# Attention and two feed-forward layers on one core: reciprocals broadcast per head, sums of exponentials on POOL, six weight chunks moved

## Chip, cores, metric

One Trainium2 chip, of which the kernel uses one core. The metric is the device time of one execution in microseconds, the median of several runs. The engines are named as in the profile: PE (matmul), PEld (its weight loads), DVE (vector), ACT (scalar), POOL (GpSimd), SP (the queue that issues the DMAs).

## What is computed

Attention over 4 batches of 8 heads with 576 positions and 64 channels (the mask is causal, a bias comes from a running sum of s), a feed-forward layer with softplus, and a gated one with an RMS norm in front. The second softmax denominator has a small constant added; the change touches where.

```python
scores = scale * np.matmul(q, k.transpose(0, 1, 3, 2))
cum = np.cumsum(np.maximum(s, 0.0), axis=-1)
bias = -(cum[:, :, :, None] - cum[:, :, None, :])
scores = np.where(causal, -1000000000.0, scores + np.minimum(bias, 0.0))
attn = np.exp(scores - np.max(scores, axis=-1, keepdims=True))
attn = attn / (np.sum(attn, axis=-1, keepdims=True) + 1e-09)
x = np.matmul(attn, v)             # then (2304, 512): tokens by channels of all heads
h = x @ w_in                       # 512 -> 2048
x = (np.maximum(h, 0.0) + np.log1p(np.exp(-np.abs(h)))) @ w_out
xn = x / np.sqrt(np.mean(x * x, axis=-1, keepdims=True) + 1e-06) * rms_g
g = xn @ w_gate                    # 512 -> 1536
return (g / (1 + np.exp(-g)) * (xn @ w_val)) @ w_out2
```

## The kernel before

The kernel has three stages. **Attention** works on 16 pairs of heads. **The first feed-forward layer** takes 96 steps: six tiles of 384 tokens by six of the sixteen blocks of hidden channels, and then the same tiles by the other ten. **The gated layer** takes 72 steps. Matmuls of single precision are done as three products of a high and a low half (mm3, lines 771 to 774), so each weight is split in two.

The weights lie in memory as float64. A *chunk* of 128 x 512 of them is fetched as 64-bit words (w_fetch, 512 KB), turned into float32 by ACT (w_conv_a, lines 246 and 247), DVE (w_conv_d, lines 253 to 257) and POOL (w_conv_p, line 263), and then either split and kept (w_hi, w_lo) or stored to memory for later (w_store, 256 KB). There are 32 chunks for the first layer and 36 for the second. While attention runs, 12 of the first and N2 = 10 of the second are converted; the remaining 20 and 26 are converted during the first feed-forward layer, the latter one in every OFF2["CV"] = 2.3 steps.

One pair of heads goes through this: q and k are loaded (a_load, line 378) into one of four buffers, two pairs deep; PE transposes them (line 396), ACT and DVE split them into high and low halves (407, 412). A first, coarse product gives scores (a_one, 449) from which DVE takes the row maxima (472); these are transposed (480), copied and put by a small DMA into the operand aq (489, 490). A second, precise product with the maxima folded in (a_two, 505) is turned into exponentials e by ACT (522). PE multiplies them with v (a_v, 539). For the denominators the blocks of e are first added up into zs (a_a, line 533): one add of 128 x 896 on POOL, one of 128 x 640 and one of 128 x 384 on DVE; PE multiplies zs with ones (a_z, also 539). ACT copies the three PSUM results into xz (a_ox, 575), values in xz[:, 0] and sums in xz[:, 1]. A DMA spreads the sums over 128 partitions (z, line 579), DVE adds 1e-9 and takes reciprocals (583, 584), a DMA writes them to memory (rd, 587), and another reads them back, each head's row into 64 partitions (rb, line 591). POOL multiplies (a_xm, 595), and a DMA stores the product x of the pair (line 599).

The order of all this is not written out. attention_ops lists every operation with engine, duration, latency, dependencies and PSUM banks (names such as LD for the load, ZD for z, ZR for the reciprocals, RS for rd, BC for rb, XM for the product, XW for its store, DM for the maxima); attention_order takes them one by one, always the one that could start first by these figures, ties going to the lower rank. The rank is 14.0 per pair plus an entry of the table OFF. Each engine and the SP queue then work through their instructions in that order, and each waits in place where an operand is not ready. SP issues all the DMAs named here. The feed-forward stages are ordered by positions in steps (OFF1, OFF2).

At the end of attention the first two steps of the feed-forward layer (h) stand between the last pairs; the loads of the next token tiles (xr, line 743) stand on SP behind the last store x.

Of the kernel before, what the change touches and what calls it, by code (L numbers as in the profile page):

```python
# [14 lines left out]
AF = mybir.ActivationFunctionType  # L15
# [29 lines left out]
    "PER": 14.0,  # L45
    "LV": -22.71,
    "QT0": 48.88,
    "QH0": -18.02,
    "QL0": -12.77,
    "QT1": 34.64,  # L50
    "QH1": 54.37,
    "QL1": -43.15,
    "AQ": -3.83,
    "RA": -2.83,
    "KA": -0.66,
    "RB": 1.61,
    "KB": -67.40,
    "RC": -33.20,
    "KC": -70.00,
    "RD": -40.04,  # L60
    "MA0": 19.65,
    "MA1": 19.98,
    "MB0": -2.10,
    "MB1": -6.43,
    "MC0": -24.56,
    "MC1": -4.25,
    "MD0": -39.54,
    "MD1": -43.39,
    "MN": 20.02,
    "MT": 9.71,  # L70
    "MH": 24.06,
    "DM": -45.58,
    "Ra": -54.93,
    "Ka": -33.43,
    "Rb": 15.22,
    "Kb": -42.71,
    "Rc": 28.54,
    "Kc": -2.10,
    "Rd": 22.47,
    "Kd": -45.39,  # L80
    "Ea0": -43.42,
    "Ea1": -31.34,
    "Eb0": -34.46,
    "Eb1": 3.11,
    "Ec0": 19.15,
    "Ec1": 24.52,
    "Ed0": -13.92,
    "Ed1": -13.58,
    "A1": 55.11,
    "A2": -55.59,  # L90
    "A3": -54.22,
    "V0": -60.16,
    "V1": -35.91,
    "Z0": -53.57,
    "Z1": 55.74,
    "O0": -58.66,
    "O1": -68.97,
    "O2": 34.39,
    "ZD": -15.00,
    "ZR": 47.90,  # L100
    "RS": -7.46,
    "BC": 47.04,
    "XM": -26.00,
    "XW": -53.74,
    "LD": 10.70,
    "CF": -5.85,
    "CA": 49.36,
    "CD": 70.00,
    "CP": -58.95,
    "CH": 24.21,  # L110
    "CL": 4.79,
    "CS": -55.59,
    "XL": 15.17,
    "X0": -12.63,
    "X1": 20.03,
    "X2": 14.37,
    "X3": 70.00,
    "H0": 5.54,
    "H1": 16.80,
}  # L120
CONV0 = 0.45
CONVR = 0.33
OFF2 = {
    "CV": 2.3,
    "L0": 84.28205,
# [31 lines left out]
def attention_moe_kernel(ctx, tc, q, k, v, s, w_in, w_out, w_gate, w_val, w_out2, rms_g, out):  # L157
# [19 lines left out]
    NA = 2 * FA  # L177
    N2 = 10
    CONV = [(1, c) for c in range(NA)] + [(2, c) for c in range(NA, NA + N2)]
# [345 lines left out]
    def a_a(p, n):  # L525
        e = st["e", p]
        if n == 0:
            st["zs", p] = pools["xo"].tile([P, 2, S - P], F32, tag="zs", name="zs", bufs=2)
        zs = st["zs", p]
        o, x, y, eng = ((zs, e[:, :, P:S], e[:, :, 832:1280], nc.gpsimd),  # L530
                        (zs[:, :, P:], zs[:, :, P:], e[:, :, 1280:1600], nc.vector),
                        (zs[:, :, 2 * P:], zs[:, :, 2 * P:], e[:, :, 576:768], nc.vector))[n]
        eng.tensor_tensor(out=o, in0=x, in1=y, op=ALU.add)

# [32 lines left out]
    def a_ox(p, part):  # L567
        if ("xz", p) not in st:
            st["xz", p] = pools["xo"].tile([P, 2, S], F32, tag="xz", name="xz", bufs=2)
        xz = st["xz", p]  # L570
        if part == 2:
            o, x = xz[:, :, IS:S], st.pop(("x1", p))[:, 0:2 * (S - IS)].rearrange("p (t s) -> p t s", t=2)
        else:
            o, x = xz[:, part, 0:IS], st.pop((("o", "oz")[part], p))[:, 0:IS]
        nc.scalar.activation(out=o, in_=x, func=AF.Copy)

# [4 lines left out]
    def a_zr(p):  # L581
        z = st["z", p]
        nc.vector.tensor_scalar(out=z, in0=z, scalar1=1e-9, scalar2=None, op0=ALU.add)
        nc.vector.reciprocal(out=z, in_=z)

    def a_rd(p):
        nc.sync.dma_start(out=rdd[p].rearrange("h (p c) -> (h p) c", c=9), in_=st.pop(("z", p)))

    def a_rb(p):
        rb = st["rb", p] = pools["xo"].tile([P, S], F32, tag="rb", name="rb", bufs=2)  # L590
        nc.sync.dma_start(out=rb, in_=rdd[p].unsqueeze(1).broadcast_to([2, D, S]))

# [9 lines left out]
    def attention_ops():  # L602
# [8 lines left out]
        for p in range(NP):  # L611
            def add(nm, eng, dur, fn, deps, p=p, **kw):
                op((nm, p), eng, dur, fn, [d if isinstance(d, tuple) else (d, p) for d in deps], p, **kw)

            def old(k, *nms, p=p):
                return [(nm, p - k) for nm in nms] if p >= k else []
# [4 lines left out]
            if p > 1:  # L621
                add("LD", "SP", 1.35, lambda p=p: a_load(p), old(2, "QT0", "QT1"), lat=2.5)
            add("LV", "SP", 1.7, lambda p=p: a_loadv(p), old(3, "V0", "V1"), lat=2.2)
            for w in range(2):
# [16 lines left out]
            add("MH", "ACT", 0.25, lambda p=p: a_mh(p), ["MT"])  # L641
            add("DM", "SP", 1.25, lambda p=p: a_md(p), ["MH", "RA", "RB", "RC", "RD"], lat=2.2)
            for bk, du, ku in (("a", 0.93, 0.11), ("b", 1.32, 0.17), ("c", 0.93, 0.11), ("d", 0.6, 0.11)):
# [16 lines left out]
            add("O1", "ACT", 0.5, lambda p=p: a_ox(p, 1), ["Z0", "O0"])  # L660
            add("O2", "ACT", 0.5, lambda p=p: a_ox(p, 2), ["V1", "Z1", "O0"])
            add("ZD", "SP", 0.62, lambda p=p: a_zd(p), ["O1", "O2"] + old(2, "RS"), lat=2.0)
            add("ZR", "DVE", 0.46, lambda p=p: a_zr(p), ["ZD"])
            add("RS", "SP", 0.35, lambda p=p: a_rd(p), ["ZR"], lat=2.0)
            add("BC", "SP", 0.62, lambda p=p: a_rb(p), ["RS"] + old(2, "XM"), lat=2.2)
            add("XM", "POOL", 1.45, lambda p=p: a_xm(p), ["BC"])
            add("XW", "SP", 0.55, lambda p=p: a_xw(p), ["XM"], lat=2.0)
        for c, (ph, ch) in enumerate(CONV):
            def cv(nm, eng, dur, fn, deps, c=c, ph=ph, ch=ch, **kw):
                op((nm, c), eng, dur, lambda: fn(ph, ch), [d if isinstance(d, tuple) else (d, c) for d in deps],  # L670
                   CONV0 + CONVR * c, **kw)

            def was(nm, k, c=c):
                return [(nm, c - k)] if c >= k else []

            cv("CF", "SP", 0.65, w_fetch, was("CD", 2), lat=5.0)
# [409 lines left out]
```

## Time and profile before

| what | us |
|---|---|
| runs | 1229.65 median of 3 (1229.56 to 1230.39) |
| the profiled execution | 1226.48, its span 1224.7 |
| PE busy | 1120.9 |
| DVE, ACT, POOL busy | 737.2, 560.4, 435.7 |

The span is the time from the first to the last instruction of the profiled execution. Attention fills its first 300 us or so, the first feed-forward layer goes to about 775 us, the gated layer to the end. An engine's busy time counts its own instructions; what it waited for is shown beside the instruction that waited, with an arrow to what released it.

### The profile page before, as it was taken

To read this page: it belongs to the slowest core of one execution; us is meant where nothing else is said; L and a number is where in the kernel's file an instruction comes from. 1 tells how busy PE (TensorE), PEld (TensorE's weight loads), DVE (VectorE), ACT (ScalarE), POOL (GpSimd) and SP (SyncE) were. 2 spreads that over 40 slices of the span, in tenths; PEclk is the share of its full clock that TensorE was granted. 3 is DMA by queue.
4 is the path that set the end of the run, shared out by engine and by line. 5 is a ranking of instruction groups with operands and counts; after the bars stand their busy time and mean duration, and the time that the engine had idled before them with its cause. 6 is when DMAs were issued, how large, how long until landed. Compare 5 with 4: busy or idle time off the path is not lost.

```text
span 1224.7 us, 19418 instructions
## 1 busy us (share of the span) xinstructions
PE 1120.9 (92%) x7428; PEld 1027.6 (84%) x7428; DVE 737.2 (60%) x1218; ACT 560.4 (46%) x1187; POOL 435.7 (36%) x372
## 2 busy tenths in 40 slices
PE   4978887889599989999989988999999999999998
PEld 4756766667588888999989888999999999999997
DVE  5667775544289999889999998433233332333322
ACT  2454544433387887777667666342121111211111
POOL 4466534322265454236567766761000000000000
PEclk9987898997799999999999999999999999999999
DMA  7364566431244343443432332431001010010000
GB/s 172 92 148 122 149 169 169 116 105 44 92 127 136 121 127 123 126 132 101 154 104 60 115 113 63 129 115 63 1 13 39 14 40 1 13 40 13 27 1 27
DMA packets 126493, 107.60 MB, mean 88 GB/s; under 512 B 66528, under 2 KB 112224, under 8 KB 126336
## 3 DMA queue, kind: packets, MB, share of 16 engines
q1 hardware_dynamic: 126368, 106.36, 29.5%
q8 instruction: 58, 0.95, 0.3%
q14 instruction: 35, 0.29, 0.1%
q0 software_dynamic: 32, 0.00, 0.0%
HBM read 80.36 MB, written 25.83 MB: 87 GB/s over the span
## 4 chain that ended last, share of the span: by engine, by line
PE 56%; DVE 22%; DMA 11%; issue 5%; ACT 3%; POOL 3%; SPq 0%; DVEq 0%; POOLq 0%; ACTq 0%
DMA kn<-in_k_dram 5%; DVE gl L824 5%; PE g L774 4%; PE g L773 4%; PE v L773 4%; PE v L774 4%; PE v L772 4%; PE g L772 4%; DVE e L807 3%; PE t L505 3%; PE o L948 3%; PE o L949 3%; PE o L947 3%; DVE l L815 3%; PE o L539 2%
## 5 line engine op out<-in xcount | busy, mean ns | idle before, releaser
L773 PE MATMUL y<-gl,w 128*128 128x384 f32 x384 | 133.9, 349 | 23.3 <-DVE gl L824 16.2
L263 POOL TENSOR_TENSOR wf<-ur 128x512 int32<-128x512 int32 x68 | 95.1, 1398 | 130.5 <-DVE ur L257 61.7
L772 PE MATMUL y<-gh,w 128*128 128x384 f32 x384 | 131.9, 343 | 4.5 <-ACT l L799 4.5
L932 DVE TENSOR_TENSOR u<-g,u 128x384 f32<-128x384 f32 x71 | 39.5, 557 | 158.4 <-ACT u L931 158.4
L774 PE MATMUL y<-gh,w 128*128 128x384 f32 x384 | 131.6, 343 | 0.0
L934 ACT ACTIVATE gh<-l 128x384 fp32r<-128x384 f32 x72 | 37.8, 524 | 156.6 <-DVE l L933 156.6
L931 ACT ACTIVATE u<-g 128x384 f32<-128x384 f32 x71 | 34.8, 491 | 151.1 <-PE g L774 151.1
L773 PEld LDWEIGHTS y<-gl,w 128*128 128x128 f32 x384 | 74.4, 194 | 29.7 <-DVE gl L824 21.4
L773 PE MATMUL g<-xl,w 128*128 128x384 f32 x284 | 95.5, 336 | 0.7 <-DVE xl L766 0.7
L824 DVE TENSOR_TENSOR gl<-l,gh 128x384 fp32r<-128x384 f32 x90 | 93.6, 1040 | 4.1 <-ACT gh L819 0.7
L807 DVE SCALAR_TENSOR_TENSOR e<-u,e 128x384 f32<-128x384 f32 x96 | 79.9, 832 | 26.7 <-ACT l L799 26.7
L774 PE MATMUL g<-xh,w 128*128 128x384 f32 x284 | 95.8, 337 | 0.0
L772 PE MATMUL g<-xh,w 128*128 128x384 f32 x284 | 95.6, 337 | 0.0
L772 PE MATMUL v<-xh,w 128*128 128x384 f32 x284 | 94.9, 334 | 0.0
L774 PE MATMUL v<-xh,w 128*128 128x384 f32 x284 | 94.9, 334 | 0.0
L773 PE MATMUL v<-xl,w 128*128 128x384 f32 x284 | 94.9, 334 | 0.0
L773 PE MATMUL h<-xl,w 128*128 128x384 f32 x256 | 86.4, 338 | 5.1 <-POOL xl L769 5.1
L522 ACT ACTIVATE e<-t 128x448 f32<-128x448 f32 (+2 forms) x128 | 57.8, 503 | 69.4 <-PE t L515 67.6
L472 DVE TENSOR_REDUCE mc<-s 128x1 f32<-128x320 f32 (+4 forms) x160 | 77.2, 536 | 17.8 <-PE s L457 14.3
L772 PE MATMUL h<-xh,w 128*128 128x384 f32 x256 | 86.7, 339 | 0.7 <-DVE e L811 0.6
L774 PE MATMUL h<-xh,w 128*128 128x384 f32 x256 | 85.6, 335 | 0.0
L815 DVE TENSOR_TENSOR l<-l,e 128x384 f32<-128x384 f32 x96 | 78.9, 822 | 3.7
(179 smaller groups left out, 3040.1 us busy)
## 6 DMA issues: line engine op xcount, KB each, us to landing
raw<-in_moe_w_out_dram SPq DMA_DIRECT2D x28, 512.0 KB
raw<-in_moe_w_in_dram SPq DMA_DIRECT2D x16, 512.0 KB
raw<-in_moe_w_gate_dram SPq DMA_DIRECT2D x12, 512.0 KB
raw<-in_moe_w_val_dram SPq DMA_DIRECT2D x12, 512.0 KB
wf<-wf SPq DMA_DIRECT2D x24, 256.0 KB
wl<-wf SPq DMA_DIRECT2D x24, 256.0 KB
xr<-x SPq DMA_DIRECT2D x28, 192.0 KB
qn<-in_q_dram SPq DMA_DIRECT2D x16, 288.0 KB
```

The source lines that it names most:

```text
L263: nc.gpsimd.tensor_tensor(out=w.bitcast(I32), in0=u, in1=r3, op=ALU.add)
L472: nc.vector.reduce_max(out=o, in_=x, axis=AX.X, negate=True)
L505: nc.tensor.matmul(t[hd][:, c:c + w], lt, rt, start=(n == 0 and a == 0), stop=(a == 3 and not diag), skip_group_check=True)
L522: nc.scalar.activation(out=st["e", p][:, hd, c:c + w], in_=st["t", p, bk][hd][:, 0:w], func=AF.Exp)
L772: nc.tensor.matmul(o, wh, xh, start=start, stop=False)
L773: nc.tensor.matmul(o, wh, xl, start=False, stop=False)
L774: nc.tensor.matmul(o, wl, xh, start=False, stop=stop)
L807: nc.vector.scalar_tensor_tensor(out=e, in0=st.pop(("u", i)), scalar=-1.0, in1=e, op0=ALU.add, op1=ALU.subtract)
L815: nc.vector.tensor_tensor(out=l, in0=l, in1=st.pop(("e", i)), op=ALU.add)
L824: eng.tensor_tensor(out=gl, in0=st.pop(("l", i)), in1=f32(st["gh", i]), op=ALU.subtract)
L932: nc.vector.tensor_tensor(out=u, in0=g, in1=u, op=ALU.mult)
L934: nc.scalar.activation(out=gh, in_=l, func=AF.Copy)
```

## The change

Four things change, and with them the planner and the order.

1. The broadcast rb is issued as two DMAs, one per head, each from one row to 64 partitions; before it was one DMA from two rows to 128.
2. All three adds of exponentials are done by POOL.
3. The constant 1e-9 is added in ACT's copy of the sums into xz; the third copy becomes two, one for the values and one for the sums, and DVE's add on z goes away.
4. Sixteen chunks of the second layer instead of ten are converted during attention; the 20 that remain come one in 2.9 steps.
5. The planner's durations and latencies are changed with these, and so is the table OFF of ranks, nearly all of its entries.

```diff
-    "LV": -22.71,
-    "QT0": 48.88,
+    "LV": 62.98,
+    "QT0": 67.58,
...
-    "CV": 2.3,
+    "CV": 2.9,
...
-    N2 = 10
+    N2 = 16
...
-        o, x, y, eng = ((zs, e[:, :, P:S], e[:, :, 832:1280], nc.gpsimd),
-                        (zs[:, :, P:], zs[:, :, P:], e[:, :, 1280:1600], nc.vector),
-                        (zs[:, :, 2 * P:], zs[:, :, 2 * P:], e[:, :, 576:768], nc.vector))[n]
-        eng.tensor_tensor(out=o, in0=x, in1=y, op=ALU.add)
+        o, x, y = ((zs, e[:, :, P:S], e[:, :, 832:1280]),
+                        (zs[:, :, P:], zs[:, :, P:], e[:, :, 1280:1600]),
+                        (zs[:, :, 2 * P:], zs[:, :, 2 * P:], e[:, :, 576:768]))[n]
+        nc.gpsimd.tensor_tensor(out=o, in0=x, in1=y, op=ALU.add)
...
-        if part == 2:
-            o, x = xz[:, :, IS:S], st.pop(("x1", p))[:, 0:2 * (S - IS)].rearrange("p (t s) -> p t s", t=2)
+        if part < 2:
+            jobs = ((part, slice(0, IS), st.pop((("o", "oz")[part], p))[:, 0:IS]),)
         else:
-            o, x = xz[:, part, 0:IS], st.pop((("o", "oz")[part], p))[:, 0:IS]
-        nc.scalar.activation(out=o, in_=x, func=AF.Copy)
+            x = st.pop(("x1", p))
+            jobs = ((0, slice(IS, S), x[:, 0:S - IS]), (1, slice(IS, S), x[:, S - IS:2 * (S - IS)]))
+        for w, c, x in jobs:
+            nc.scalar.activation(out=xz[:, w, c], in_=x, func=AF.Copy, bias=(0.0, 1e-9)[w])
...
-        nc.vector.tensor_scalar(out=z, in0=z, scalar1=1e-9, scalar2=None, op0=ALU.add)
         nc.vector.reciprocal(out=z, in_=z)
...
-        nc.sync.dma_start(out=rb, in_=rdd[p].unsqueeze(1).broadcast_to([2, D, S]))
+        for hd in range(2):
+            nc.sync.dma_start(out=rb[half(hd)], in_=rdd[p][hd].unsqueeze(0).broadcast_to([D, S]))
...
-                add("LD", "SP", 1.35, lambda p=p: a_load(p), old(2, "QT0", "QT1"), lat=2.5)
+                add("LD", "SP", 1.3, lambda p=p: a_load(p), old(2, "QT0", "QT1"), lat=4.0)
...
-            add("A2", "DVE", 0.72, lambda p=p: a_a(p, 1), ["A1", "Ed0", "Ed1"])
-            add("A3", "DVE", 0.46, lambda p=p: a_a(p, 2), ["A2"])
+            add("A2", "POOL", 1.6, lambda p=p: a_a(p, 1), ["A1", "Ed0", "Ed1"])
+            add("A3", "POOL", 1.0, lambda p=p: a_a(p, 2), ["A2"])
...
-            add("BC", "SP", 0.62, lambda p=p: a_rb(p), ["RS"] + old(2, "XM"), lat=2.2)
-            add("XM", "POOL", 1.45, lambda p=p: a_xm(p), ["BC"])
+            add("BC", "SP", 1.0, lambda p=p: a_rb(p), ["RS"] + old(2, "XM"), lat=3.5)
+            add("XM", "POOL", 1.42, lambda p=p: a_xm(p), ["BC"])
```

What the order becomes, at two places. First SP's queue, from one broadcast to the store rd of the next pair's reciprocals. Before, at pair 7 (rd7; the numbers are buffers, x1 is the output of batch 1):

```order
L591 DMA rb_2668<-rd7_82 128x1x576
L378 DMA qn_2675<-in_q_dram 96x12x64
L378 DMA kn_2677<-in_k_dram 96x12x64
L267 DMA wf2_108<-wf_2670 128x512
L385 DMA vn2_145<-in_v_dram 128x4x64 x2
L388 DMA vn2_145<-in_v_dram 64x2x64
L599 DMA x1_92<-xz_2412 128x576
L579 DMA z_2793<-xz_2664 128x1x9
L238 DMA raw_2799<-in_moe2_w_gate_dram 128x4x128
L267 DMA wf2_108<-wf_2797 128x512
L587 DMA rd8_83<-z_2793 128x9
```

And now, at pair 6:

```order
L593 DMA rb_2642<-rd6_81 64x576 x2
L378 DMA qn_2666<-in_q_dram 96x12x64
L378 DMA kn_2668<-in_k_dram 96x12x64
L581 DMA z_2733<-xz_2573 128x1x9
L238 DMA raw_2751<-in_moe2_w_gate_dram 128x4x128
L601 DMA x1_92<-xz_2320 128x576
L385 DMA vn2_145<-in_v_dram 128x4x64 x2
L388 DMA vn2_145<-in_v_dram 64x2x64
L588 DMA rd7_82<-z_2733 128x9
L238 DMA raw_2821<-in_moe2_w_val_dram 128x4x128
L489 DMA aq_2377<-mt_2768 2x4x128
```

The sums z of the next pair stand ahead of the store x of this one, which needs rb; before, they stood behind it. The load of q and k that stands behind rb is used by PE's transposes of the coming period in the order before, and of the period after that now. The stores wf of converted chunks have moved in front of rb, behind the maxima aq (out of these rows).

Second, POOL's queue over one pair. Before (aq is the scaling at line 418, e the exponentials, wf a conversion, xz times rb the product):

```order
L418 TENSOR_SCALAR aq_2082<-all10_153,oh_128 128x576
L533 TENSOR_TENSOR zs_2129<-e_1976 128x896
L263 TENSOR_TENSOR wf_2166<-ur_2034 128x512
L595 TENSOR_TENSOR xz_1908<-xz_1908,rb_2164 128x576
L263 TENSOR_TENSOR wf_2293<-ur_2168 128x512
```

And now:

```order
L418 TENSOR_SCALAR aq_2630<-all10_153,oh_128 128x576
L533 TENSOR_TENSOR zs_2714<-e_2545 128x896
L597 TENSOR_TENSOR xz_2320<-xz_2320,rb_2642 128x576
L263 TENSOR_TENSOR wf_2765<-ur_2672 128x512
L533 TENSOR_TENSOR zs_2714<-zs_2714,e_2545 128x2x320
L263 TENSOR_TENSOR wf_2823<-ur_2753 128x512
L533 TENSOR_TENSOR zs_2714<-zs_2714,e_2545 128x2x192
```

The product, which waits for rb, stands between the first add and the two that have come from DVE.

## Rows read from the trace of the kernel before

**Rows 1.** The page, part 1: busy us, share of the span, instructions.

```profile
PE 1120.9 (92%) x7428; PEld 1027.6 (84%) x7428; DVE 737.2 (60%) x1218; ACT 560.4 (46%) x1187; POOL 435.7 (36%) x372
```

**Rows 2.** Stretches: length, PE PEld DVE ACT POOL busy, clock, DMA share, GB/s.

```profile
56.09:288.94 232.85, 194.86 (x2253) 152.22 (x2251) 147.37 (x307) 106.68 (x250) 100.22 (x77) 0.87 0.49 133
...
475.00:775.00 300.00, 284.00 (x1582) 279.65 (x1583) 270.25 (x378) 209.28 (x431) 179.65 (x149) 0.98 0.36 112
```

**Rows 3.** Waits of PE, 0 to 330 us: total us, times, longest.

```profile
PE qkT L396 <- DMA kn<-in_k_dram: 28.9, 11, 6.9
PE s L449 <- DVE hl L412: 12.4, 5, 4.7
```

**Rows 4.** Timeline of SP's queue: start us, us to issue.

```profile
86.59 0.68 SPq L378 DMA_DIRECT2D kn<-in_k_dram  x1
...
195.73 0.52 SPq L591 DMA_DIRECT2D rb<-rd  x1
...
197.04 4.37 SPq L378 DMA_DIRECT2D kn<-in_k_dram  x1
...
207.16 0.54 SPq L599 DMA_DIRECT2D x<-xz  x1
207.80 0.59 SPq L579 DMA_DIRECT2D z<-xz  x1
...
210.84 0.34 SPq L587 DMA_DIRECT2D rd<-z  x1
...
213.77 0.50 SPq L591 DMA_DIRECT2D rb<-rd  x1
```

**Rows 5.** Timeline of POOL and DVE in the same period: idle before, its releaser.

```profile
205.15 1.40 POOL L595 TENSOR_TENSOR xz<-xz,rb 128x576 f32<-128x576 f32 x1 [10.04 <-DMA rb<-rd]
...
209.94 0.63 DVE L583 TENSOR_SCALAR z<-z 128x9 f32<-128x9 f32 x1 [6.78 <-DMA z<-xz]
```

**Rows 6.** The chain that ended last, two broadcasts: start us, us.

```profile
104.27 9.37 DMA rb<-rd
...
317.47 7.68 DMA rb<-rd
```

**Rows 7.** A stretch inside the second of them, columns as in rows 2.

```profile
319.40:320.40 1.00, 1.00 (x5) 1.00 (x4) 0.00 (x0) 0.00 (x0) 0.00 (x0) 0.50 0.13 51
```

**Rows 8.** Three periods of attention, columns as in rows 2.

```profile
96.87:118.68 21.81, 17.97 (x175) 13.88 (x171) 15.83 (x28) 8.78 (x20) 15.37 (x13) 0.71 0.54 149
...
184.88:203.49 18.61, 15.46 (x173) 11.79 (x172) 11.20 (x25) 8.76 (x20) 6.67 (x5) 0.82 0.59 165
...
238.26:252.58 14.32, 12.35 (x176) 9.78 (x172) 7.98 (x19) 6.34 (x16) 4.18 (x3) 1.00 0.40 103
```

**Rows 9.** POOL's groups to 500 us; DVE and POOL on zs, 56.09 to 288.94.

```profile
L263 POOL TENSOR_TENSOR wf<-ur 128x512 int32<-128x512 int32 x44 | 60.9, 1383 | 63.6 <-DVE ur L257 29.7 <-ACT e L791 14.6 <-ACT w L289 4.9
...
L533 POOL TENSOR_TENSOR zs<-e 128x896 f32<-128x896 f32 x16 | 34.9, 2178 | 5.3 <-issue 4.6 <-POOL xz L595 0.7
...
56.09:288.94 232.85, 19.23 (x112) 7.28 (x112) 22.93 (x26) 28.38 (x13) 0.87 0.49 133
```

**Rows 10.** 475 to 775: conversion tile ur (DVE, ACT, POOL busy); a wait of PE.

```profile
475.00:775.00 300.00, 49.42 (x78) 31.83 (x52) 37.50 (x27) 0.98 0.36 112
...
PE y L773 <- DVE gl L824: 8.3, 7, 2.9
```

**Rows 11.** Timeline of PE and SP at the end of attention.

```profile
306.85 0.28 PE L539 MATMUL x<-e,low 128*64 128x64 f32 x4
...
312.84 0.53 SPq L579 DMA_DIRECT2D z<-xz  x1
...
316.47 0.69 PE L772 MATMUL x<-xh,w 128*128 128x384 f32 x1 [9.34 <-DVE e L811]
...
326.80 0.32 SPq L599 DMA_DIRECT2D x<-xz  x1
...
327.77 0.54 PE L773 MATMUL y<-gl,w 128*128 128x384 f32 x1 [4.55 <-POOL gl L824]
```

More of the change, by code (lines that the diff above doesn't have):

```diff
@@ L45 @@
     "PER": 14.0,
-    "LV": -22.71,
-    "QT0": 48.88,
[L48 to L107, printed above, removed]
-    "CD": 70.00,
[L109 to L119, printed above, removed]
+    "LV": 62.98,
+    "QT0": 67.58,
+    "QH0": -47.10,
+    "QL0": 22.87,
+    "QT1": -35.92,
+    "QH1": -31.98,
+    "QL1": -29.18,
@@ new lines @@
+    "AQ": -9.63,
+    "RA": 22.45,
+    "KA": -34.18,
+    "RB": 23.95,
+    "KB": -47.44,
+    "RC": 8.43,
+    "KC": -45.90,
+    "RD": -5.20,
+    "MA0": -29.89,
+    "MA1": 49.55,
+    "MB0": 5.96,
+    "MB1": -18.45,
+    "MC0": 15.47,
+    "MC1": -10.82,
+    "MD0": -29.27,
+    "MD1": -69.58,
+    "MN": 38.85,
+    "MT": -17.13,
+    "MH": 19.92,
+    "DM": -35.34,
+    "Ra": -53.72,
+    "Ka": 21.68,
+    "Rb": 41.97,
+    "Kb": -65.15,
+    "Rc": 51.95,
+    "Kc": -19.10,
+    "Rd": 49.86,
@@ new lines @@
+    "Kd": -32.26,
+    "Ea0": 67.23,
+    "Ea1": 15.50,
+    "Eb0": -19.75,
+    "Eb1": -70.00,
+    "Ec0": 27.14,
+    "Ec1": -15.92,
+    "Ed0": -70.00,
+    "Ed1": -22.07,
+    "A1": -70.00,
+    "A2": -15.37,
+    "A3": -60.92,
+    "V0": 26.07,
+    "V1": 25.88,
+    "Z0": 17.33,
+    "Z1": -58.69,
+    "O0": 65.54,
+    "O1": -26.63,
+    "O2": 0.99,
+    "ZD": 1.55,
+    "ZR": 44.29,
+    "RS": -55.71,
+    "BC": 49.74,
+    "XM": -34.27,
+    "XW": -15.37,
+    "LD": 67.85,
+    "CF": -17.81,
@@ L120 @@
+    "CA": 38.15,
+    "CD": 70.00,
+    "CP": -45.96,
+    "CH": -21.20,
+    "CL": 38.62,
+    "CS": 31.87,
+    "XL": 54.95,
+    "X0": -39.99,
+    "X1": -65.50,
+    "X2": -18.52,
+    "X3": -56.07,
+    "H0": 56.97,
+    "H1": -70.00,
 }
@@ L621, in attention_ops @@
             if p > 1:
-                add("LD", "SP", 1.35, lambda p=p: a_load(p), old(2, "QT0", "QT1"), lat=2.5)
-            add("LV", "SP", 1.7, lambda p=p: a_loadv(p), old(3, "V0", "V1"), lat=2.2)
+                add("LD", "SP", 1.3, lambda p=p: a_load(p), old(2, "QT0", "QT1"), lat=4.0)
+            add("LV", "SP", 1.7, lambda p=p: a_loadv(p), old(3, "V0", "V1"), lat=4.0)
             for w in range(2):
@@ L641, in attention_ops @@
             add("MH", "ACT", 0.25, lambda p=p: a_mh(p), ["MT"])
-            add("DM", "SP", 1.25, lambda p=p: a_md(p), ["MH", "RA", "RB", "RC", "RD"], lat=2.2)
+            add("DM", "SP", 1.25, lambda p=p: a_md(p), ["MH", "RA", "RB", "RC", "RD"], lat=2.7)
             for bk, du, ku in (("a", 0.93, 0.11), ("b", 1.32, 0.17), ("c", 0.93, 0.11), ("d", 0.6, 0.11)):
@@ L660, in attention_ops @@
             add("O1", "ACT", 0.5, lambda p=p: a_ox(p, 1), ["Z0", "O0"])
[L661 to L664, printed above, removed]
-            add("BC", "SP", 0.62, lambda p=p: a_rb(p), ["RS"] + old(2, "XM"), lat=2.2)
-            add("XM", "POOL", 1.45, lambda p=p: a_xm(p), ["BC"])
+            add("O2", "ACT", 0.68, lambda p=p: a_ox(p, 2), ["V1", "Z1", "O0"])
+            add("ZD", "SP", 0.62, lambda p=p: a_zd(p), ["O1", "O2"] + old(2, "RS"), lat=2.3)
+            add("ZR", "DVE", 0.25, lambda p=p: a_zr(p), ["ZD"])
+            add("RS", "SP", 0.35, lambda p=p: a_rd(p), ["ZR"], lat=2.4)
+            add("BC", "SP", 1.0, lambda p=p: a_rb(p), ["RS"] + old(2, "XM"), lat=3.5)
+            add("XM", "POOL", 1.42, lambda p=p: a_xm(p), ["BC"])
             add("XW", "SP", 0.55, lambda p=p: a_xw(p), ["XM"], lat=2.0)
@@ L674, in was @@
                 return [(nm, c - k)] if c >= k else []
-            cv("CF", "SP", 0.65, w_fetch, was("CD", 2), lat=5.0)
+            cv("CF", "SP", 0.65, w_fetch, was("CD", 2), lat=6.0)
             cv("CA", "ACT", 1.35, w_conv_a, ["CF"] + was("CP", 2))
-            cv("CD", "DVE", 1.6, w_conv_d, ["CA"])
+            cv("CD", "DVE", 1.85, w_conv_d, ["CA"])
             cv("CP", "POOL", 1.28, w_conv_p, ["CD"] + ([("CL" if c - 3 < NA else "CS", c - 3)] if c > 2 else []))
             if ph == 1:
-                cv("CH", "POOL", 0.62, w_hi, ["CP"])
-                cv("CL", "POOL", 1.28, w_lo, ["CH"])
+                cv("CH", "POOL", 0.7, w_hi, ["CP"])
+                cv("CL", "POOL", 1.38, w_lo, ["CH"])
             else:
```

## The prediction

> **What bounds the kernel now.** I read the page first, then a table of stretches, then the waits and the queues of the worst stretch. PE is busy for 92% of the span [rows 1], so only stages where it is not busy can give much. From 56.09 to 288.94 us, 13 pairs of heads of the attention stage, PE is idle for 232.85 - 194.86 = 38.0 us [rows 2] and its granted clock is 0.87 of full speed on the mean; from 475 to 775 us, in the first feed-forward layer, it is idle for only 16.0 us [rows 2]. Behind 775 us nothing of the change runs.
>
> What PE waits for in attention is a load: transposes wait for kn for 28.9 us, for the low half hl for 12.4 [rows 3]. But a late load has a cause on its queue. [rows 4] is one period of SP's queue, which works strictly in order. The broadcast rb is issued at 195.73. The load of k behind it takes 4.37 us to issue, where at 86.59 it took 0.68. The store x of the pair (XW) goes out at 207.16 only, since it needs POOL's product, which starts at 205.15 after 10.04 us of idling for rb [rows 5]. Behind XW stand the sums z (207.80), which land for DVE at 209.94, their reciprocals rd (210.84), and the next broadcast at 213.77. That is a closed ring: 195.73 to 213.77 is 18.04 us, and the mean period is 232.85 / 13 = 17.91. **The ring of the reciprocals sets the pace of attention**, and 9.42 us of it is the landing of rb.
>
> Why does rb take so long? Not for traffic: with the DMA engines otherwise idle it took 7.68 us [rows 6], and in that time the 16 DMA engines were busy for a share of 0.13, which is two of them, moving 51 GB/s [rows 7]. Its source is two rows of sums, and two engines copy each of them 64 times: 294,912 bytes at 51 GB/s are 5.8 us, so 1.9 us is the rest.
>
> **The broadcast per head.** Each of the two DMAs now has 64 copies of one row as its outer dimension, so I expect all 16 engines to take part: 5.8 x 2 / 16 = 0.7 us of moving, 2.6 alone with the rest; 0.5 for the second issue (one takes 0.50 [rows 4]) and 1.7 for traffic (9.42 - 7.68) give 4.9 us. No row shows this DMA; the ends are 2.6 us and the 9.42 of now, and I take 4.9 because the two engines are seen and the added terms too. What argues against issuing halves at all is a rule of the Trainium skill, DMA: Bandwidth & Descriptors, Rules for kernel authors: two transfers to disjoint halves of the partitions serialize on the same 16 engines, so one should not bother. The same section says that the slowest dimension of size above 1 limits the engines, a leading broadcast of c copies to c of them. The trace agrees with the second, two engines in [rows 7]; by the first alone the change would give nothing here, which is the second rival.
>
> **The order.** In the new order z of the next pair stands ahead of XW, so the ring loses the landing of z; it is at most the landing of rb + product 1.40 + 0.61 to XW + 3.68 from XW to rd + 2.93 from rd to rb [rows 4, 5], landing + 8.6. With 4.9 that is 13.5 us. The loads of q and k, now issued 8 to 10 us before PE wants them, go out a period earlier, so I let the whole kn wait go. What is late next is PE itself and POOL.
>
> **PE per pair.** Its busy time was 15.46 us in a period with two conversions, 12.35 in one without at an undisturbed pace [rows 8]. I take 13.9, between them, since stretches without stalls show the higher clock, and 0.7 for waits that stay (those for hl are 12.4 / 13 = 1.0 now): 14.6.
>
> **The adds on POOL.** DVE spent 22.93 us on 26 adds, 1.76 a pair; POOL takes 2178 ns for 896 columns, 2.43 ns each, so the two moved adds cost it 1.56 + 0.93 = 2.49 a pair [rows 9]. DVE is not the bound in attention (11.20 of 18.61 us [rows 8]), so its gain counts nothing. POOL late in the stage: first add 2.18, product 1.40, two conversions of 1.38, moved adds 2.49, together 8.8 of a period of 14.6, and PE wants the sum only at the period's end: cover enough. Early, where POOL also splits weights, it was busy 15.37 us in one period [rows 8], and 17.9 would be too much. For the four early periods I therefore take 16.5, between the 14.6 of PE and 17.9. The notes are harsher: the Trainium skill, GPSIMD Engine Reference, Engine selection, calls GpSimd about half as fast as VectorE for elementwise work on two inputs. By it the moved adds would be 3.5 us a pair; the rows above make it 1.4 times.
>
> So 4 x 16.5 + 9 x 14.6 = 197.4 us against 232.85: **-35.4 us**.
>
> **The copy with the constant.** One ACT instruction more per pair (0.44 on the mean, 8.76 us in 20 [rows 8]); ACT is busy under half of a period, so 0 here, and at most 16 x 0.44 = 7 us if ACT were the bound. DVE's add on nine columns goes (0.63 [rows 5]), in the shadow of the landing of z: 0.6 us in the tail alone, inside its rounding.
>
> **Six chunks moved.** In attention each costs between 0 and half of the 3.1 us by which the two PE figures of [rows 8] differ, most of which the term for PE holds already: **+2 us** for the last pairs, which had none. In the feed-forward stretch DVE does 49.42 us of conversion for 26 chunks, 1.90 each [rows 10]; six fewer leave it 11.4 of 270.25 us less. PE's idle time there, 16.0 us, of which 8.3 wait for gl from DVE, bounds the gain; 6/26 of it is 3.7: **-4 us**.
>
> **The tail.** The last attention matmul ends at 307.13, its XW goes out at 326.80 [rows 11]. In front of its z stood the XW of the pair before: z left at 312.84. PE lost 9.34 us there behind DVE, whose queue held the reciprocal, and 4.55 us behind POOL, whose queue held the last product. With z ahead of that XW 5 us go, with a fast rb another 7.68 - 3.1 = 4.6; since the two last broadcasts now come close together I take **-9 us**, of 0 to 14.
>
> **Sum.** -35.4 + 2 - 4 - 9 = -46.4 us. The profiled execution took 1226.48 us (span 1224.7), 3.2 under the median of 1229.65; against the median, 1183 us.
>
> **Rivals.**
> 1. *POOL is the bound.* The chain add, product, conversion, add, conversion, add stands in one queue, and the product in it waits for rb. For it: 15.37 + 2.49 us early. Against it: 8.8 us later. If early periods stay at 19 and the later ones take 15.5, attention gains 232.85 - 215.5 = 17 us: 1229.65 - 17 + 2 - 4 - 9, about 1201 us.
> 2. *The halves land no sooner* (9.4 us). The ring is then 9.4 + 8.6 = 18.0, as long as now; the tail gains its 5 us and the feed-forward layer 4: about 1222 us. [rows 7] speaks against it, but that the engines follow the outer dimension is my reading.
> 3. *Slower: one engine per broadcast.* Two engines and two source rows fit just as well to one engine per row of the source. Then each half has one row and one engine, the same one for both: 11.6 us of moving, landing 11.6 + 1.9 + 1.7 = 15.2. The ring is 23.8, +5.9 us in each of 13 periods, so 1229.65 + 77 - 4 = about 1302 us. It decides as soon as the landing exceeds 17.9 - 8.6 = 9.3 us.
> 4. *No change*: the gains are eaten by new stalls of the rewritten order, such as DVE's reciprocal, which now stands ahead of reductions that PE waits for.
>
> **How the numbers follow.** 0.2% of the time is 2.5 us, about what a measurement of this kernel can tell from none. Chances: forecast 0.72, rival 1 0.12, rival 2 0.07, rival 3 0.06, rival 4 0.03. The forecast's own range: 13.6 us in every period (PE 12.9, near its undisturbed 12.35) and the whole 14 us of the tail make 1229.65 - 56 + 2 - 4 - 14 = 1158; 16.5 us in every period and half the tail 1205. The range 1158 to 1216 holds it and rival 1 with some room, and leaves rivals 2 and 3 out. Faster 0.91, same 0.03, slower 0.06.
>
> **What would show it.** Right: POOL's wait for rb falls from 10 us to under 4, issues of k take 0.7 us, no transposes wait for kn, the 13 periods take 14 to 16 us at a clock above 0.87, and the tail shrinks. Wrong: rb lands in 7 us or more; or PE waits for zs from POOL; or DVE's reductions wait behind the reciprocal; or the stretch 475 to 775 keeps its length.

## The result and the profile after

The changed kernel takes 1172.79 us (median of 4 runs, 1171.22 to 1175.72) against 1230.02 us for the kernel before on the same chip: a ratio of 0.9537, interval 0.9516 to 0.9558. 1183 us were predicted, in a range of 1158 to 1216. The profiled execution took 1173.68 us, 52.8 less than the one before; the medians lie 57.2 us apart, since the median before is 3.5 us above its profiled execution and the one now 0.9 below.

Busy time in all has changed little: PE has lost 13 us, DVE 6, and POOL has gained 39 (the page, part 1, against [rows 1]):

```profile
PE 1108.0 (95%) x7428; PEld 1021.9 (87%) x7428; DVE 731.3 (62%) x1170; ACT 560.5 (48%) x1203; POOL 474.8 (41%) x404
```

Two stretches of the changed kernel, columns as in [rows 2]. The first is the same 13 pairs of heads, from the transpose of the maxima of the third pair to that of the sixteenth; the second goes from the first output matmul y of the first feed-forward layer that takes the low half gl to the first matmul g of the gated one. (The one y in front of it ran at 322.88 in the kernel before, ahead of PE's wait for POOL of [rows 11]; with this mark that wait counts to the end of attention.)

```profile
48.38:248.89 200.51, 186.62 (x2220) 149.44 (x2218) 165.50 (x285) 112.36 (x273) 141.76 (x109) 0.88 0.68 175
285.71:709.88 424.17, 401.88 (x2242) 391.79 (x2242) 379.21 (x538) 312.86 (x655) 240.15 (x192) 0.99 0.34 108
```

The same second stretch of the kernel before:

```profile
327.77:763.20 435.43, 405.70 (x2241) 395.26 (x2242) 395.51 (x556) 319.87 (x667) 249.25 (x198) 0.98 0.37 117
```

The 13 pairs take 200.51 us instead of 232.85, with PE idle for 13.9 us instead of 38.0. PE's last attention matmul ends at 272.98 instead of 307.13 (-34.2), the y with gl starts 7.9 us sooner after it, the layer is 11.3 us shorter, and that is the gain: 53.3 us at the first g. The gated layer is unchanged.

The broadcasts, from the chain that ended last, against 9.37 and 7.68 [rows 6]. These rows start at the second of the two issues; from the first one it is 0.5 us more:

```profile
251.90 2.98 DMA rb<-rd
...
278.49 2.96 DMA rb<-rd
```

Half a microsecond inside the second, where [rows 7] had a DMA share of 0.13 and 51 GB/s (here the store of the pair before runs beside it):

```profile
280.50:281.00 0.50, 0.50 (x4) 0.50 (x3) 0.00 (x0) 0.00 (x0) 0.00 (x0) 0.50 0.93 327
```

In the middle of attention, where other transfers run, a broadcast and POOL's product that waits for it look like this:

```profile
148.84 1.45 SPq L593 DMA_DIRECT2D rb<-rd  x2
...
154.19 1.88 POOL L597 TENSOR_TENSOR xz<-xz,rb 128x576 f32<-128x576 f32 x1 [0.88 <-DMA rb<-rd]
```

From issue to product it is 5.35 us, where [rows 4, 5] had 9.42.

SP's queue over a period (timeline: start us, us to issue), with the rows that answer to [rows 4]:

```profile
162.68 1.51 SPq L593 DMA_DIRECT2D rb<-rd  x2
...
164.93 0.98 SPq L378 DMA_DIRECT2D kn<-in_k_dram  x1
...
169.35 0.58 SPq L581 DMA_DIRECT2D z<-xz  x1
...
171.78 0.46 SPq L601 DMA_DIRECT2D x<-xz  x1
...
178.31 1.36 SPq L593 DMA_DIRECT2D rb<-rd  x2
```

The load of k behind the broadcast issues in 0.98 us, where it took 4.37. PE's waits up to 330 us (total, times, longest), against [rows 3]:

```profile
PE qkT L396 <- DMA kn<-in_k_dram: 11.2, 3, 6.7
PE x L774 <- DVE e L813: 5.6, 1, 5.6
PE qkT L396 <- DVE hl L412: 3.8, 1, 3.8
PE qkT L396 <- issue: 3.8, 1, 3.8
PE t L505 <- DVE mc L472: 3.3, 5, 1.0
PE s L449 <- DVE hl L412: 2.7, 1, 2.7
```

Of eleven waits for kn three are left, and these end before 31 us; from 45 us on the kernel before has

```profile
PE qkT L396 <- DMA kn<-in_k_dram: 17.2, 8, 3.1
```

and the changed kernel none. The 12.4 us for hl have become 2.7. POOL waits for rb for 15.0 us in 8 times, 1.9 us on the mean; in the kernel before it was 125.2 us in 14 times.

The last stores x of attention in SP's queue, two issues in one row, against 326.80 [rows 11]; the second ends with the row:

```profile
279.40 3.98 SPq L601 DMA_DIRECT2D x<-xz  x2
```

### The profile page after: what moved, and what is told of

Its sections match the earlier page's. It is cut to its first block, busy times and chain, and to the rows that moved or that the text cites. A ratio compares the mean times of both kernels' runs of the same rounds, so it can differ in the third digit from the quotient of the medians.

```text
span 1171.5 us, 19408 instructions
## 1 busy us (share of the span) xinstructions
PE 1108.0 (95%) x7428; PEld 1021.9 (87%) x7428; DVE 731.3 (62%) x1170; ACT 560.5 (48%) x1203; POOL 474.8 (41%) x404
## 4 chain that ended last, share of the span: by engine, by line
PE 59%; DVE 25%; issue 4%; DMA 4%; ACT 4%; POOL 3%; SPq 0%; DVEq 0%; POOLq 0%; ACTq 0%
DVE gl L826 4%; PE g L776 4%; PE g L775 4%; PE v L774 4%; PE v L775 4%; PE v L776 4%; PE g L774 4%; PE t L505 3%; DVE ur L253 3%; DVE l L817 3%; PE o L950 3%; PE o L951 3%; DVE ur L255 3%; PE s L449 3%; PE o L949 3%
## 5 line engine op out<-in xcount | busy, mean ns | idle before, releaser
L775 PE MATMUL y<-gl,w 128*128 128x384 f32 x384 | 131.5, 342 | 14.9 <-DVE gl L826 12.4
L774 PE MATMUL y<-gh,w 128*128 128x384 f32 x384 | 129.8, 338 | 2.2 <-DVE yt L853 1.8
L776 PE MATMUL y<-gh,w 128*128 128x384 f32 x384 | 129.4, 337 | 0.0
L472 DVE TENSOR_REDUCE mc<-s 128x1 f32<-128x128 f32 (+4 forms) x160 | 76.7, 537 | 31.6 <-PE s L457 25.9
L826 DVE TENSOR_TENSOR gl<-l,gh 128x384 fp32r<-128x384 f32 x90 | 88.3, 981 | 4.5 <-ACT gh L821 1.0
```

The lines of the kernel that those rows point to most:

```text
L472: nc.vector.reduce_max(out=o, in_=x, axis=AX.X, negate=True)
L774: nc.tensor.matmul(o, wh, xh, start=start, stop=False)
L775: nc.tensor.matmul(o, wh, xl, start=False, stop=False)
L776: nc.tensor.matmul(o, wl, xh, start=False, stop=stop)
L826: eng.tensor_tensor(out=gl, in0=st.pop(("l", i)), in1=f32(st["gh", i]), op=ALU.subtract)
```

## The experiments

The question was which part of the change made the gain. Medians and ratios with their intervals are of the runs; "end" is where PE's last attention matmul ends in the profiled execution, "layer" the time from the first y with gl to the first g, us.

| kernel | broadcast | order | adds | chunks | median | ratio to before | end | layer |
|---|---|---|---|---|---|---|---|---|
| before | one DMA | old | DVE | 10 | 1230.02 | 1 | 307.13 | 435.4 |
| after | per head | new | POOL | 16 | 1172.79 | 0.9537 (0.9516 to 0.9558) | 272.98 | 424.2 |
| e1 | per head | old | DVE | 10 | 1177.97 | 0.9575 (0.9541 to 0.9610) | 264.06 | 433.0 |
| e2 | one DMA | new | POOL | 16 | 1224.52 | 0.9939 (0.9918 to 0.9960) | 314.09 | 426.5 |
| e3 | per head, outer 2 | new | POOL | 16 | 1235.91 | 1.0034 (1.0017 to 1.0052) | 323.87 | 426.0 |
| e4 | per head | new | DVE | 16 | 1169.54 | 0.9504 (0.9476 to 0.9532) | 268.05 | 425.4 |
| e5 | per head | new | POOL | 10 | 1177.08 | 0.9572 (0.9525 to 0.9618) | 262.15 | 433.4 |
| e6 | one DMA | old | DVE | 16 | 1238.33 | 1.0063 (1.0038 to 1.0089) | 330.93 | 426.0 |
| e7 | per head | old | DVE | 16 | 1179.35 | 0.9590 (0.9555 to 0.9625) | 279.79 | 424.8 |
| e8 | per head, outer 4 | new | POOL | 16 | 1193.41 | 0.9700 (0.9664 to 0.9737) | 285.89 | 427.3 |
| e9 | per head | new | DVE | 10 | 1176.44 | 0.9547 (0.9523 to 0.9571) | 265.35 | 436.0 |
| e10 | per head, constant | old | DVE | 10 | 1171.97 | 0.9514 (0.9488 to 0.9540) | 263.05 | 435.6 |
| e11 | after once more | | | | 1172.39 | 0.9513 (0.9484 to 0.9542) | 276.05 | 424.7 |
| e12 | e4 once more | | | | 1166.94 | 0.9486 (0.9460 to 0.9513) | 266.34 | 424.8 |

e1 to e4, e5 to e8 and e9 to e12 each ran as one set. "New" order means the new table and planner figures; with it goes the constant at the copy. An end is that of one execution: after and e11, the same kernel, differ by 3.1 us in it, and the profiled execution was 5.7 us under its median in e1 and 4.1 in e5, 5.0 above it in e6 and 4.8 in e11. So ends alone do not settle differences of a few microseconds.

### The broadcast alone, and the rest without it (e1, e2)

e1 is the kernel before with one edit; e2 takes the same edit out of the changed kernel:

```diff
-        nc.sync.dma_start(out=rb, in_=rdd[p].unsqueeze(1).broadcast_to([2, D, S]))
+        for hd in range(2):
+            nc.sync.dma_start(out=rb[half(hd)], in_=rdd[p][hd].unsqueeze(0).broadcast_to([D, S]))
```

> The kernel before with one edit: the broadcast issued per head; order, adds, copy and conversions as before. Ring theory (the landing of rb paces attention, and a broadcast whose outer dimension is 64 uses all engines): rb lands in about 3 us alone, the ring of 18.0 us shrinks to about 13.5, PE sets the pace at 15 to 16 us, so 25 to 35 us go in the 13 periods and about 5 in the tail, where z still stands behind the store of the pair before: 1192 to 1200 us. Order theory (the rewritten order makes the gain, the broadcast little): 1222 to 1230 us.

> The changed kernel with the one DMA of two rows put back; order, adds on POOL, copy and conversions as changed. Ring theory: rb lands in 7.7 us alone and 9 to 10 beside other transfers, the ring is about 18 us again, attention loses 25 to 33 us and the tail about 5: 1203 to 1212 us. Order theory: the new order, with z ahead of the store, hides the slow broadcast: 1173 to 1182 us.

The one edit takes the ratio to 0.9575; everything else without it comes to 0.9939. So the broadcast per head makes nearly the whole gain, more of it than I gave it, and the order far less: both times lie outside what I expected of the ring theory, e1 14.0 us below the range and e2 12.5 us above. In e1 the second of the last two broadcasts moves without another store beside it, and the share of the DMA engines is 0.70, more than eleven of sixteen:

```profile
270.00:270.50 0.50, 0.50 (x3) 0.50 (x2) 0.31 (x1) 0.00 (x0) 0.00 (x0) 0.50 0.70 212
```

In e2 the ring is as long as before although z no longer stands behind XW. SP's queue and the reciprocal on DVE show why:

```profile
168.72 0.54 SPq L592 DMA_DIRECT2D rb<-rd  x1
...
170.04 4.61 SPq L378 DMA_DIRECT2D kn<-in_k_dram  x1
174.92 3.24 SPq L581 DMA_DIRECT2D z<-xz  x1
...
179.77 0.33 SPq L600 DMA_DIRECT2D x<-xz  x1
180.19 1.08 SPq L385 DMA_DIRECT2D vn<-in_v_dram  x2
181.32 0.65 SPq L388 DMA_DIRECT2D vn<-in_v_dram  x1
182.06 0.56 SPq L588 DMA_DIRECT2D rd<-z  x1
...
186.35 0.52 SPq L592 DMA_DIRECT2D rb<-rd  x1
```

```profile
180.55 0.22 DVE L585 RECIPROCAL z<-z 128x9 f32<-128x9 f32 x1 [3.29 <-DMA z<-xz]
```

Behind the slow broadcast the load of k takes 4.61 us to issue and z, which stood in front of XW to go early, another 3.24; in the changed kernel the same two issues take 0.98 and 0.58. A slow DMA holds up the queue behind it as well. But that is not what keeps the ring long: the reciprocals are ready at 180.77, and their store rd goes out at 182.06 only. In the new order, too, rd stands behind XW, with the loads of v in between, and then it is 4.29 us to rb, where it was 2.93, since the maxima aq and the stores wf now stand in front of rb. From XW to rb that is 6.58 us, where it was 3.68 + 2.93 = 6.61 [rows 4], and from rb to rb 17.63.

### Engines, or number of DMAs (e3, e8)

Two DMAs per pair as in the change, but each written with 2 (e3) or 4 (e8) as its outer dimension:

```diff
-            nc.sync.dma_start(out=rb[half(hd)], in_=rdd[p][hd].unsqueeze(0).broadcast_to([D, S]))
+            nc.sync.dma_start(out=rb[half(hd)],
+                              in_=rdd[p][hd].unsqueeze(0).unsqueeze(0).broadcast_to([4, D // 4, S]))
```

> The changed kernel, still two DMAs per pair, one per head, but each with its 64 copies written as 2 x 32 in the source, so that its outer dimension is 2. If the engines follow the outer dimension of the source: two engines, rb lands in 7 to 8 us alone, and the time is that of the one DMA, 1203 to 1214 us. If it is the number of DMAs, or the 64 partitions of the target, that counts: 1172 to 1176 us, rb in 3 us.

> The changed kernel, each head's broadcast written with an outer dimension of 4 and 16 copies inside. Theory (engines follow the outer dimension): four engines take part, the two broadcasts land in 4.5 to 5 us alone and 6 to 7 beside other traffic, the ring is 15 to 16 us, and the time 1174 to 1190 us. Rival (any broadcast that leaves engines out holds up the queue behind it): landing 8 to 9 us and the time above 1215 us, as with an outer dimension of 2.

With an outer dimension of 2 the gain is gone. The chain that ended last in e3, and a stretch inside the second of these:

```profile
75.07 8.99 DMA rb<-rd
...
308.31 8.92 DMA rb<-rd
```

```profile
310.00:311.00 1.00, 1.00 (x7) 1.00 (x7) 0.00 (x0) 0.51 (x3) 1.00 (x1) 1.00 0.13 39
```

Two engines again (0.13 of 16), and 9 us. (Another broadcast stands in the chain with 2.99 us, and behind it 5.89 in which POOL waits for nothing that the profile shows: 8.9 again up to the product.) With 4 (e8), chain and stretch:

```profile
76.81 5.77 DMA rb<-rd
...
293.79 5.63 DMA rb<-rd
```

```profile
297.00:298.00 1.00, 1.00 (x7) 1.00 (x6) 0.00 (x0) 0.00 (x0) 0.00 (x0) 1.00 0.25 90
```

0.25 of 16 is four engines, at 90 GB/s. The dose is plain: landings of about 9, 5.7 and 3 us behind the second issue, medians of 1235.91, 1193.41 and 1172.79. So it is the outer dimension that sets the engines; two DMAs as such gain nothing (e3 is slower than e2, which has one). The 1236 of e3 is 22 us above what I expected of the engine theory, the 1193 of e8 3 us. The Trainium skill, DMA: Bandwidth & Descriptors, Rules for kernel authors, says that an outermost dimension of c below 16 confines a DMA to at most c engines; the trace agrees at outer dimensions of 2 and 4 (shares of 0.13 and 0.25), and with 64 the share is above both (0.70 in e1). The rule there that two transfers to disjoint halves are not worth it holds for e3 against e2, and not for this change, whose halves have another outer dimension than the whole.

### The adds (e4, e12, e11)

```diff
-        nc.gpsimd.tensor_tensor(out=o, in0=x, in1=y, op=ALU.add)
+        (nc.gpsimd if n == 0 else nc.vector).tensor_tensor(out=o, in0=x, in1=y, op=ALU.add)
```

> The changed kernel with the second and third add of exponentials back on DVE, at the same places of the order. My theory (the adds are off the path on either engine; POOL's 2.5 us a pair are covered): 1170 to 1178 us, PE's waits for zs under 5 us in total. Rival (DVE, at 165 of 200 us in the stretch, is near its bound, and relief of it is part of the gain): 1180 to 1190 us, PE waiting longer for reductions and low halves.

> The changed kernel with the second and third add on DVE once more, beside it. Theory (the adds on POOL cost 3 to 5 us): 3 to 5 us under the changed kernel of the same set, 1167 to 1171 us. Rival (the difference seen before was one between chips or sessions): within 1 us of it.

> The changed kernel once more, for a comparison on the same chip as the two around it: 1170 to 1176 us.

(The planner still counts the two adds as POOL's, so the order stays.) With them back on DVE the kernel is 3.3 us faster in one set against the result's median (half a microsecond below the range I expected) and 5.5 us in the other, where both ran; end of attention 4.9 and 9.7 us sooner. The intervals of the ratios overlap in both sets, so the runs favour, without quite settling, that the move to POOL is a loss. POOL spent 2.66 us a pair on the two adds, where 2.49 was forecast, DVE 1.63 in e12, and the move relieved DVE of little. DVE's groups of the conversion up to 275 us, first of the changed kernel, then of e12 (busy us, mean ns):

```profile
L253 DVE TENSOR_SCALAR ur<-ur 128x512 f32<-128x512 f32 x28 | 35.9, 1282 | 0.0
...
L255 DVE TENSOR_SCALAR ur<-ur 128x512 int32<-128x512 int32 x28 | 25.4, 907 | 1.0
L257 DVE SCALAR_TENSOR_TENSOR ur<-raw,ur 128x512 int32<-128x512 int32 x28 | 24.2, 863 | 1.0
```

```profile
L253 DVE TENSOR_SCALAR ur<-ur 128x512 f32<-128x512 f32 x28 | 24.4, 872 | 0.0
...
L257 DVE SCALAR_TENSOR_TENSOR ur<-raw,ur 128x512 int32<-128x512 int32 x28 | 22.3, 795 | 1.0
L255 DVE TENSOR_SCALAR ur<-ur 128x512 int32<-128x512 int32 x28 | 21.5, 767 | 1.0
```

The same 84 instructions take 85.5 us instead of 68.2; of the 26.1 us that the 32 adds cost DVE in e12, 17.3 are given back. Why, two timelines tell. DVE and then POOL of the changed kernel:

```profile
169.03 1.52 DVE L255 TENSOR_SCALAR ur<-ur 128x512 int32<-128x512 int32 x1
...
172.77 1.67 DVE L253 TENSOR_SCALAR ur<-ur 128x512 f32<-128x512 f32 x1
174.48 0.43 DVE L255 TENSOR_SCALAR ur<-ur 128x512 int32<-128x512 int32 x1
```

```profile
168.73 1.54 POOL L597 TENSOR_TENSOR xz<-xz,rb 128x576 f32<-128x576 f32 x1
171.35 1.29 POOL L263 TENSOR_TENSOR wf<-ur 128x512 int32<-128x512 int32 x1 [1.09 <-DVE ur L257]
172.60 1.56 POOL L533 TENSOR_TENSOR zs<-zs,e 128x640 f32<-128x640 f32 x1
```

The conversion at 172.77 starts under POOL's add and ends at 174.44, 0.28 us behind the add's end at 174.16; the one at 169.03 ends 0.28 us behind the product. Line 255 takes 0.43 us where POOL does nothing. Up to 275 us this is so for 39 of the 84 conversion instructions: each of them ends 0.27 to 0.29 us (line 257: 0.54 to 0.56) behind the POOL instruction under which it began, and every other one of a line takes the same 0.42, 0.43 or 0.69 us. In the kernel before 16 of 66 were held up, 6 of the 22 of line 253; in e12 26 of 84, 15 of the 28 of line 253; in the changed kernel 23 of these 28. The Trainium skill has the rule, SBUF — State Buffer, Who interferes with whom: VectorE and GpSimd share a pair of ports, which a VectorE instruction needs in a two-port mode or with two inputs in SBUF; the first to issue then has the pair for its whole instruction, and the other is blocked until then. The trace agrees, with 0.28 us to resume, and in both directions: the product at 154.19 begins 0.10 us into an instruction of line 257 and takes 1.88 us, where its shortest takes 1.41. That the blocking is the whole cost of the moved adds was not tried.

### The six chunks (e5, e6, e7, e9)

```diff
-    "CV": 2.9,
+    "CV": 2.3,
...
-    N2 = 16
+    N2 = 10
```

e5 is the changed kernel with this, e6 the kernel before with the reverse, e7 the same on e1, and e9 is e4 with it.

> The changed kernel with the chunk count set back (ten chunks of the second layer in attention, 26 in the first layer, one in 2.3 steps). Theory (the moved chunks are what shortens the first layer): from the first to the last output matmul of that layer it takes 444 to 449 us again instead of 437, and attention, with six conversions fewer, ends 2 to 9 us sooner, so 1172 to 1180 us in all. Rival (the layer gained by another part of the change): the layer stays at 436 to 439 us and the whole comes to 1164 to 1172.

> The kernel before with sixteen chunks in attention, nothing else; the broadcast stays one DMA. Theory (the ring of the reciprocals paces attention, so six more conversions there hide in its waits, and the first layer gains 9): 1220 to 1224 us against about 1231. Rival (what the first layer gains attention pays): 1228 to 1236.

> The kernel before with the broadcast per head and sixteen chunks in attention; adds, constant and order table as before. Theory (with a fast broadcast DVE and PE bound attention, so six more conversions cost there 4 to 9 us, about what the first layer gains): 1172 to 1179 us, beside 1178 with ten chunks. Rival (the chunks are a gain by themselves): 1165 to 1170.

> The changed kernel with two parts undone: the second and third add on DVE again, and ten chunks in attention again. What is left of the change: the broadcast per head, the constant at the copy, the new order. Theory (the adds on POOL cost attention some 5 us, the six chunks are a wash): attention's last matmul ends at 256 to 259 us, the first layer takes 433 to 435 us, the whole 1166 to 1171 us, a little under the changed kernel. Rival (with ten chunks DVE has the work that the adds bring back only by waiting, so the two do not add up): 1172 to 1178 us.

The chunks are what shortens the layer: 433 to 436 us in every kernel with ten, 424 to 427 in every one with sixteen, whatever else differs. What attention pays for them is not the same everywhere. By the ends it is 23.8 us in the kernel before (307.13 to 330.93), 15.7 with the fast broadcast in the old order (e1 to e7), 10.8 and 13.9 in the new order with the adds on POOL (e5 to after and e11), 2.7 and 1.0 in the new order with the adds on DVE (e9 to e4 and e12). But the profiled executions of e1, e5, e6 and e11 are the ones that lie off their medians. By the ratios, at 1232 us, and the layer's gain, my estimate is 17, 10, 1 to 5 and 4 to 5 us, uncertain by about 3 us in the first and 4 to 6 in the others, going by the intervals. That shows the slow broadcast to be dear; it does not tell the adds on POOL from those on DVE.

In sum e6 is slower than before, above even its rival, so my theory that the conversions hide in the waits of the ring fell; e7 is no faster than e1; after and e11 are 4 to 5 us below e5 and e4 and e12 7 to 10 below e9. Of these gains only that of e12 is clear of the intervals. Clear of them too is e7 against e4 and e12, all with the fast broadcast, sixteen chunks and the adds on DVE: 0.9590 against 0.9504 and 0.9486, 11 to 13 us. So with sixteen chunks the new order and the constant are worth something together; no run has the old order with both the constant and sixteen chunks, so the share of each stays open. e9 did not come out where the theory put it: undoing the adds and the chunks together gave 1176.44 us, as its rival said, with attention ending at 265.35 where 256 to 259 was expected. With ten chunks the adds on POOL (e5) cost nothing against those on DVE (e9): 1177.08 and 1176.44 us, ends of 262.15 and 265.35.

### The constant at the copy, and the order (e10)

The change of a_ox and a_zr, as in the diff of the change, on e1:

> The kernel before with the broadcast per head and the constant added at the copy (two copies for the third, no add on nine columns on DVE); order, adds and chunks as before. Theory (a gain in the tail alone): within 2 us of the 1178 us with the broadcast per head alone, and attention's last matmul within 2 us of 263.8 us. Rival (the copies are on the path, 0.3 to 0.44 us for each of 16 pairs): 1181 to 1186 us.

In the profiles e10 ends attention 1.0 us sooner than e1, as expected, and the spans are 1170.3 and 1170.5 us; but e1's was its fastest execution. The medians lie 6.0 us apart, where 2 were expected, in different sets, and the intervals nearly touch; what the constant is worth stays open. What e10 does show: with the broadcast per head and the constant, in the old order, with the old adds and the old chunks, the kernel is as fast (0.9514) as with the whole change (0.9513 in the same set). e9, which differs from e10 by the new order alone, is not faster (0.9547; attention ends at 265.35 against 263.05).

## Why the prediction came out right, step by step

**The ring of the reciprocals bounds attention, and the landing of rb is its largest piece: right**, shown by e1. The landing from the first issue was put at 4.9 us, 3.1 of it without traffic; in the changed kernel it is 5.35 to the product at 154.19, and 3.46 for the last broadcast. So was the reading that the outer dimension sets the engines, by which rivals 2 and 3 fell (e3, e8).

**The order as a gain for the ring: wrong.** The step "in the new order z of the next pair stands ahead of XW, so the ring loses the landing of z" leaves out that rd still stands behind XW, now with the loads of v in between, and that aq and the stores wf have come between rd and rb: in e2 XW to rb takes 6.58 us instead of 6.61, and the ring 17.63. Its bound, landing + 8.6, did hold; by it rival 2 put the ring with a slow landing at 18.0. With a fast broadcast the old order does as well: e10, in which POOL still waits for rb 13 times, 53.9 us, is no slower than e9. What the new order brings, with the constant, shows with sixteen chunks only (e4 and e12 against e7).

**Attention in all, -35.4 + 2 = -33.4: measured -34.2, in part by luck.** The 13 pairs gave -32.3 (232.85 to 200.51), 3.1 less than forecast. What lies before and behind them, where +2 stood, gave -1.8: -7.7 up to the transpose of the third pair (56.09 to 48.38), +5.9 from that of the sixteenth to PE's last attention matmul (18.19 to 24.09). The two errors cancel. The first points at the chunks; with ten of them (e5) the same 13 pairs take

```profile
45.60:235.92 190.32, 177.30 (x2186) 141.68 (x2184) 145.11 (x263) 100.71 (x251) 129.68 (x101) 0.92 0.63 159
```

The failing step for the chunks is "most of which the term for PE holds already": it priced them by PE's figures of [rows 8]. By the profiles the six cost 10.8 us, though e5's was a fast execution and my estimate from the ratios is 1 to 5. That their cost is DVE's work, which the moved adds made longer, fits the held-up conversions, but no run shows that it is the reason.

That DVE's gain from the adds "counts nothing" came true in another way: there was next to no gain to count, 165.50 us of DVE now and 167.77 in the same 13 pairs of e4.

```profile
45.47:245.33 199.86, 185.43 (x2220) 148.58 (x2218) 167.77 (x310) 110.87 (x272) 111.98 (x81) 0.90 0.67 175
```

Rival 1, POOL as the bound, fell: PE waits for no zs from POOL; POOL's added work shows in DVE instead. The clock of the 13 pairs, which I expected above 0.87, is only 0.88, while e1 has 0.96 in them:

```profile
49.55:246.87 197.32, 178.28 (x2251) 142.11 (x2252) 160.13 (x312) 106.61 (x252) 100.79 (x77) 0.96 0.66 159
```

That POOL's work lowers the clock is not shown: with the adds back on DVE it is 0.90 in e4 and 0.94 in e12.

**kn: right in the 13 pairs,** where all 17.2 us of its waits are gone, but not for the reason given. The step let them go because the loads go out a period earlier; in e1, with the old order, no wait for kn is left from 45 us on either. Nor were they what bounded attention: e2 has none from 45 us on, and its 13 pairs take as long as before:

```profile
53.64:286.34 232.70, 197.63 (x2219) 159.79 (x2218) 155.04 (x284) 111.79 (x272) 136.02 (x107) 0.82 0.57 150
```

The 11.2 us that are left in the changed kernel, counted into the 28.9 of [rows 3], lie ahead of the 13 pairs.

**The tail, -9: right in size, half wrong in its reason.** The last XW is issued by 283.38, 10.4 us behind the last attention matmul, where it was 20.0 (326.80 + 0.32 - 307.13): -9.6. PE sees 7.9 of it. But the step gave 5 us to z ahead of XW and 4.6 to the fast rb, and the broadcast alone does it all: from PE's last attention matmul to the y with gl it was 20.6 us before and is 12.7 now, 10.9 in e1, where z still stands behind XW, and 20.9 in e2, where it stands ahead. First e1 and e2, then the chain of e2, where rd lands slowly behind the broadcast of the pair before:

```profile
274.94 0.33 PE L774 MATMUL y<-gl,w 128*128 128x384 f32 x1
```

```profile
334.95 0.69 PE L774 MATMUL y<-gl,w 128*128 128x384 f32 x1 [8.62 <-POOL gl L825]
```

```profile
316.93 6.57 DMA rd<-z
323.56 8.84 DMA rb<-rd
```

**The first layer, -4: mis-sized, -11.3.** The step took 6/26 of PE's idle time of 475 to 775 us, 16.0. The rows of the whole layer say that DVE lost 16.3 us of work (395.51 to 379.21), PE's idle time fell by 7.4 (29.7 to 22.3) and PE's own busy time by 3.8. Almost the whole price of six conversions, 6 x 1.90 = 11.4 us by [rows 10], came back. The failing step is the share: the gain was not 6/26 of PE's idle time but near the whole of DVE's price. It looks as if DVE sets the pace of that layer, although before PE was busy for 93% of it and DVE for 91%; no run tried that.

The 10 us by which the forecast was high are chiefly this term (7.3) and 4.1 us in which the profiled executions lie off the medians (3.2 below before, 0.9 above now).

## What to carry to other kernels

When a small DMA lands late, look at the share of the engines while it is in flight: here 0.13 said two of sixteen, and another outer dimension was worth 52 us (e1). Before an order is changed to shorten a ring, follow every step of the ring through the new queue: z came forward here, and rd behind it did not. After such a ring is gone, price the other edits anew and one by one: of this change the broadcast gave nearly all, and e4, which leaves the adds on DVE, has the lowest ratios measured (0.9504 and 0.9486), though not clear of the noise. Before elementwise work is moved from DVE to POOL, see which DVE instructions will run beside it, for these may take back what the move gives.

## What was not expected of the hardware

- A DMA that uses two engines holds up those behind it on its queue: the load of k took 4.61 us to issue and the small z after it 3.24 us in e2, 0.98 and 0.58 in the changed kernel, and the small rd at the end of attention landed in 6.57 us in e2, in 2.14 in the changed kernel.
- A DVE instruction of the conversion that begins under a POOL instruction ends a fixed 0.28 us (line 257: 0.55) behind it, in 39 of 84 cases, and may so take 2.2 us instead of 0.42; POOL's own mean for its add of 896 columns, 2115 ns now and 2178 before [rows 9], shows no such price, but its product does, 1547 ns now and 1405 before.
- Two broadcasts with an outer dimension of 2 (e3) land no sooner than one on two (8.9 and 8.8 us), and the share of 0.13 shows two engines for both.
